# Layer-norm sums in float32r, gMLP weights converted ahead of time, and ten score units on half rows in an attention, feed-forward and gMLP kernel

## The chip, the core and the metric

The kernel runs on one core of a Trainium2 chip. Its time is the device time of one execution in microseconds, and a version is judged by the median of several runs. The profile is one execution of its own, recorded instruction by instruction.

## What is computed

Four batches of 448 tokens pass through soft-capped attention (12 heads of 64), a layer norm with a feed-forward part that is added to its input, and a gMLP block. All inputs and outputs are float32.

```python
scores = cap * tanh(scale * q @ k.T / cap)
x = (softmax(scores) @ v).transpose(0, 2, 1, 3).reshape(B, S, 768)
xn = (x - mean(x)) / sqrt(var(x) + 1e-06) * g_ln
x = x + relu(xn @ w_ch1) @ w_ch2                      # 768 -> 3072 -> 768
u, v = split(relu(x @ w_in))                          # 768 -> 512 + 512
v_n = (v - mean(v)) / sqrt(var(v) + 1e-06)
v_s = einsum('ts,bsd->btd', w_spatial, v_n) + b_spatial
out = (u * v_s) @ w_out                               # 512 -> 768
```

## The kernel before

**Precision.** A float32 matmul takes several passes of TensorE. For nearly all products the kernel instead splits both operands into a high and a low part in float32r and sums three matmuls (high by high, high by low, low by high; `mm3`, L547). The weights arrive as 64-bit numbers. `weight` (L566) loads one into a `w6` buffer, makes a float32 of it in a `wr` buffer (one step on ScalarE, three on VectorE), stores that in DRAM (`kept`) for the second use, and splits it into a `wh` buffer. There are two `w6`, two `wr` and three `wh` buffers. The second time the weight is used, the stored float32 is loaded and only split.

**Stages.** Work goes by pairs of batches. The lead computes attention of batches 0 and 1 with nothing else to do. Then come the feed-forward units of this pair, 24 hidden blocks in six groups: `h_units` (L977) make four hidden blocks per batch of 18 matmuls each, `y_units` (L989) add them to six output blocks, 12 matmuls each. Attention of batches 2 and 3 is spread between these units by `drive` (L1004) and `attend` (L1016). Then `gmlp` (L945) runs for the pair: products with `w_v` (`v_mm`, L846) and `w_u`, the spatial product (`sp_units`, L898) and the output product (`o_units`, L931). Feed-forward and gMLP of the second pair follow, with no attention beside them.

**Attention.** A unit is two heads, whose q and k (transposed) lie on partitions 0 to 63 and 64 to 127. `emit_s` (L643) makes the transposed scores of 128 keys at a time, in float32, one head on each half of the array's rows at the same time: chunks 0 and 1 together, chunk 2 later, each into a `two` tile (two banks of PSUM). The last 64 keys of two units are done together by `emit_st` (L656). ScalarE takes tanh and exp. `emit_v` (L705) multiplies with v and sums the exponentials, and `invert` (L676) passes these sums through DRAM to get reciprocals on all partitions. `emit_n` (L750) scales the result and adds it up in `acc`, from which the norm's mean is taken.

**Layer norm.** `ln_mean` (L769) sums `acc` over the partitions with a float32 matmul against ones, subtracts the mean, splits the centered values into `xn`, and adds up squares. `ln_scale` (L792) sums the squares by four small float32 matmuls (two instructions each) that write two columns, takes the root on GpSimd, and spreads the standard deviation over all partitions by DMA. x is multiplied by it before the products of `y_units` are added.

**Order.** All operations are first recorded, and `order` and `plan` (L251, L287) write out the order of every engine by simulating costs that are given in `Recorder`. An operation's due time is the amount of TensorE's work recorded before it, or, for others, that of its earliest user less a share of the way to it. A ready operation with the lowest due time goes first if the buffers it needs are free; none is started more than 28 us (`AHEAD`) before its due time. On the chip every engine then runs its own list in that order and waits where the plan was too optimistic. There are four `bank` and two `two` tiles for results of TensorE, 16 `rs`, 8 `rb`, 10 `hs` and 7 `es` buffers. All DMAs are issued on SP's queue.

Of the kernel before, what the change touches and what calls it, by code (L numbers as in the profile page):

```python
# [10 lines left out]
F32 = mybir.dt.float32  # L11
# [37 lines left out]

REBASE = 2.0 ** -112  # L50

EARLY = 2
# [410 lines left out]
def attn_ffn_gmlp_kernel(  # L463
# [49 lines left out]
    ones32 = const.tile([128, 2], F32, name="ones32")  # L513
    capt = const.tile([128, 1], F32, name="capt")
# [46 lines left out]
    def make(kind, j):  # L561

        with prog.early():
            made[kind, j] = weight(kind, j, [rs.get().rearrange("p a n -> p (a n)") for _ in range(2)])

    def weight(kind, j, home=None):  # L566
        if (kind, j) in made:
            return made.pop((kind, j))
# [7 lines left out]
        else:  # L576
# [5 lines left out]
            A.activation(out=t, in_=hi.bitcast(F32), func=ACTF.Copy, scale=REBASE)  # L582
# [7 lines left out]
            SP.dma_start(out=d, in_=t)  # L590
        if home:
            hi, lo = (x[:, 0:n] for x in home)
        else:
            o = (rb if j == 4 else rs).get()[:, :, 0:n] if kind == "ws" else wh.get()[:, :, 0:n]
            hi, lo = o[:, 0], o[:, 1]
        cp(hi, t, (A, V))
# [46 lines left out]
    def emit_s(i, cs):  # L643

        t = raws[i]
        scs = [twos.get()[:, :, 0:S] for _ in cs]
# [6 lines left out]
        for sc in scs:  # L653
            st.setdefault(i, []).append(expo(sc, es.get()))

# [112 lines left out]

    def ln_mean(b):  # L769

        ps = banks.get()[:, 0:S]
        T.matmul(out=ps, lhsT=ones32[:, 0:1].broadcast_to([128, 128]), rhs=accs[b % 2], start=True, stop=True)
        mean, sq = hs.get(), hs.get()
        A.activation(out=mean, in_=ps, func=ACTF.Copy, scale=1.0 / DM)
# [15 lines left out]
    def ln_scale(b):  # L792
        sq = ln.pop(b).rearrange("p (n c) -> p c n", c=NCT)
        ps = banks.get()
        with prog.group():
            for c in range(NCT):
                T.matmul(out=ps[0:CT, 2 * c:2 * c + 2], lhsT=sq[:, c], rhs=ones32, start=True, stop=True)
        var, rstd = (t[0:CT] for t in tok_t[b % 2])
        V.tensor_scalar(out=var, in0=ps[0:CT, 0:2 * NCT].rearrange("p (c t) -> p c t", t=2)[:, :, 0],
                        scalar1=1.0 / DM, scalar2=1e-6, op0=ALU.mult, op1=ALU.add)  # L800
# [45 lines left out]
    def v_mm(cs):  # L846

        two = [twos.get(), twos.get()]
        os = [banks.get() for _ in range(4)] + [t[:, j] for t in two for j in range(2)]
        os = os[:len(cs)]  # L850
        for k in range(KD):
            hi, lo = weight("wv", k)
            yh, yl = (t.rearrange("p a n -> p (a n)") for t in ysp[k])
            with prog.group():
                for c, o in zip(cs, os):
                    d = slice(c * 128, (c + 1) * 128)
                    for m, (l, r) in enumerate(((yh[:, d], hi), (yh[:, d], lo), (yl[:, d], hi))):
                        T.matmul(out=o, lhsT=l, rhs=r, start=(k == 0 and m == 0), stop=(k == KD - 1 and m == 2))
# [72 lines left out]
    def o_units(b, dt, ws):  # L931

        pss = [banks.get()[:, 0:S] for _ in ws]
        n = len(gs[b])
        with prog.group():
            for k, g in enumerate(gs[b]):
# [8 lines left out]
    def gmlp(bs, nxt):  # L945
# [16 lines left out]
        if nxt:  # L962
            ln_mean(first)
        vn.clear()
        for dts in ([0, 1, 2], *([dt] for dt in range(3, KD))):
            w = [weight("wo", dt) for dt in dts]
            for b in bs:
# [3 lines left out]
                else:  # L971
                    o_units(b, dts[0], w)
        gs.clear()
        if second:
            ln_mean(second)

    def h_units(bs, g, n):  # L977
# [3 lines left out]
        for m in steps:  # L981
            w = [weight("w1", j0 + j) for j in range(m)]
            j0 += m
            for b in bs:
                for j in range(m):
                    h_unit(b, w[j])
                    yield 3 * KD

    def y_units(bs, g, last):  # L989
# [3 lines left out]
        for b in bs:  # L993
            if b in ln:
                ln_scale(b)
# [20 lines left out]
    def attend(first, n, per):  # L1016
        todo = []
        for j in range(0, n, 2):
# [3 lines left out]
            stages = [(0.0, emit_s, i, (0, 1)), (0.1, emit_s, i, (2,)), (LOAD_QK, emit_load, i + 4),  # L1022
# [15 lines left out]
    def main():  # L1038
# [6 lines left out]
        P.memset(ones32, 1.0)  # L1045
        P.memset(mhalf, -0.5)
# [3 lines left out]
        lead = attend(0, 2 * H, 1.0) + [(H + 2.25, ln_mean, (0,)), (2 * H + 2.25, ln_mean, (1,))]  # L1050
# [73 lines left out]
```

## Time and profile before

| | |
|---|---|
| median of 3 runs | 1110.94 us (1109.65 to 1113.84) |
| the profiled execution | 1113.14 us, span of its instructions 1111.4 us |
| TensorE matmul, busy | 1094.4 us (98%), 5380 instructions |
| VectorE, busy | 704.7 us (63%) |
| ScalarE, busy | 415.6 us (37%) |
| mean granted clock of TensorE | 0.995 of full speed |

Engines are named PE (matmuls), PEld (weight loads, beside PE), DVE (VectorE), ACT (ScalarE), POOL (GpSimd) and SPq (the queue from which DMAs are issued). A row such as `bank<-rs,wh 128*128 128x448 f32` names the output tile, the operands' tiles, rows by columns of the array, and the moving operand; float32r operands are shown as f32 there. A float32 matmul stands as two instructions. All lines of the helper that records the operations are L455. Busy time counts an instruction from start to end; matmuls overlap, so the step from one start to the next is what one costs in a row.

### The profile page before, as it was taken

What the parts mean: (1) busy time and instruction counts of PE and PEld (TensorE: products, weight loads), DVE (VectorE), ACT (ScalarE), POOL (GpSimd) and SP (SyncE); (2) the same over time, 40 slices, a digit from 0 to 9 for tenths busy, and PEclk for the clock granted to TensorE, in tenths of its full rate; (3) what the DMA queues carried; (4) which work ended last, traced back from release to release, by engine and by line L of the source; (5) the groups of instructions that cost most, each with busy time, mean ns of one, the idle gap of its engine ahead of it and who ended that gap; (6) DMA issues with size and microseconds to landing.
All of it is one profiled execution on the core that took longest, in us unless ns stands there. A gap on an engine that the chain in (4) does not pass through costs nothing.

```text
span 1111.4 us, 14151 instructions
## 1 busy us (share of the span) xinstructions
PE 1094.4 (98%) x5380; PEld 899.6 (81%) x5380; DVE 704.7 (63%) x1183; ACT 415.6 (37%) x615; POOL 11.1 (1%) x17
## 2 busy tenths in 40 slices
PE   8989899999999999999999999999999999999998
PEld 2323597987888878978788899999999999998988
DVE  4768789676595776958989964533343433383861
ACT  7978743545334443354444440111111111120412
POOL 0000000000000000000001000000000000000100
PEclk9989999999999999999999999999999999999999
DMA  6545354555654564554475442212121212122303
GB/s 177 126 103 147 121 154 164 173 163 171 171 174 136 158 210 139 165 162 135 152 233 189 157 142 65 67 39 76 38 76 39 67 38 76 45 62 85 102 10 109
DMA packets 80128, 133.88 MB, mean 120 GB/s; under 512 B 35598, under 2 KB 47804, under 8 KB 80060
## 3 DMA queue, kind: packets, MB, share of 16 engines
q1 hardware_dynamic: 80060, 132.98, 40.0%
q8 instruction: 42, 0.69, 0.3%
q14 instruction: 26, 0.21, 0.1%
HBM read 100.91 MB, written 32.03 MB: 120 GB/s over the span
## 4 chain that ended last, share of the span: by engine, by line
PE 92%; DMA 4%; ACT 1%; SPq 1%; DVE 1%; issue 0%; DVEq 0%
PE bank L455 86%; PE two L455 6%; DMA inv<-rc 1%; DMA rc<-sum 1%; DMA hs<-inv 1%; SPq L455 1%; ACT es L455 1%; DMA qk<-in_qk_dram 1%; DMA w<-in_w_dram 1%; ACT hs L455 1%; DMA vt<-in_v_dram 0%; DVE acc L455 0%; DVE x L455 0%; DVE es L455 0%; ACT wr L455 0%
## 5 line engine op out<-in xcount | busy, mean ns | idle before, releaser
L455 PE MATMUL bank<-rs,wh 128*128 128x448 f32 x2232 | 451.5, 362 | 0.0
L455 PEld LDWEIGHTS bank<-rs,wh 128*128 128x128 f32 x2232 | 417.8, 187 | 33.6 <-ACT wr L455 2.8
L455 PE MATMUL bank<-rb,wh 128*128 128x448 f32 x1728 | 350.7, 363 | 0.0
L455 PEld LDWEIGHTS bank<-rb,wh 128*128 128x128 f32 x1728 | 324.8, 188 | 25.1 <-DVE hs L455 3.3
L455 DVE TENSOR_TENSOR x<-bank,x 128x448 f32<-128x448 f32 x144 | 89.5, 623 | 97.5 <-PE bank L455 96.5
L455 ACT ACTIVATE wh<-wr 128x512 fp32r<-128x512 f32 (+1 forms) x89 | 63.2, 710 | 207.4 <-PE bank L455 170.9
L455 ACT ACTIVATE rb<-bank 128x448 fp32r<-128x448 f32 x96 | 52.2, 544 | 222.4 <-PE bank L455 222.3
L455 DVE SCALAR_TENSOR_TENSOR rb<-bank,rb 128x448 fp32r<-128x448 f32 x96 | 59.8, 624 | 112.3 <-ACT rb L455 111.9
L455 DVE TENSOR_TENSOR wh<-wr,wh 128x512 fp32r<-128x512 f32 (+1 forms) x150 | 117.4, 782 | 10.7 <-ACT wh L455 6.0
L455 DVE SCALAR_TENSOR_TENSOR wr<-w,wr 128x512 int32<-128x512 int32 (+1 forms) x152 | 119.2, 785 | 2.2
L455 ACT ACTIVATE wr<-w 128x512 f32<-128x512 f32 (+1 forms) x76 | 57.6, 758 | 84.1 <-DVE wh L455 35.6
L455 ACT ACTIVATE es<-two,qsc 128x896 f32<-128x896 f32 x72 | 70.9, 1009 | 24.7 <-PE two L455 24.4
L455 PE MATMUL two<-qk 64*128 64x448 f32 x288 | 69.6, 584 | 4.2 <-DMA qk<-in_qk_dram 4.2
L455 ACT ACTIVATE es<-es,capt 128x896 f32<-128x896 f32 x72 | 72.2, 1043 | 0.0
L455 DVE CAST wh<-wr 128x512 fp32r<-128x512 f32 (+1 forms) x61 | 28.8, 472 | 66.0 <-PE bank L455 48.6
L455 PE MATMUL bank<-es,vt 128*64 128x448 f32 x288 | 63.8, 557 | 0.5 <-DMA vt<-in_v_dram 0.5
L455 PEld LDWEIGHTS two<-qk 64*128 64x128 f32 x288 | 25.0, 191 | 42.6 <-issue 22.3
L455 DVE TENSOR_TENSOR es<-es,es 128x896 f32<-128x896 f32 x48 | 52.0, 1083 | 3.5 <-ACT es L455 3.2
L455 PEld LDWEIGHTS bank<-es,vt 128*64 128x64 f32 x288 | 18.1, 137 | 41.1 <-issue 30.0
L455 ACT ACTIVATE hs<-bank 128x448 f32<-128x448 f32 x49 | 26.5, 541 | 64.2 <-PE bank L455 63.6
L455 DVE TENSOR_SCALAR wr<-wr 128x512 int32<-128x512 int32 (+1 forms) x76 | 35.8, 471 | 22.8 <-ACT wr L455 22.6
L455 PE MATMUL bank<-wh,rs 128*128 128x512 f32 x144 | 35.6, 395 | 0.0
(79 smaller groups left out, 620.0 us busy)
## 6 DMA issues: line engine op xcount, KB each, us to landing
w<-in_w_dram SPq DMA_DIRECT2D x24, 768.0 KB, 5.3
w<-in_w_dram SPq DMA_DIRECT2D x36, 512.0 KB, 4.1
qk<-in_qk_dram SPq DMA_DIRECT2D x48, 224.0 KB, 3.4
kept_w<-wr SPq DMA_DIRECT2D x24, 384.0 KB, 4.9
kept_w<-wr SPq DMA_DIRECT2D x36, 256.0 KB, 4.2
wr<-kept_w SPq DMA_DIRECT2D x24, 384.0 KB, 3.9
wr<-kept_w SPq DMA_DIRECT2D x36, 256.0 KB, 2.7
out_dram<-hs SPq DMA_DIRECT2D x24, 224.0 KB, 2.1
```

Of the source, the lines that this page charges most:

```text
L455: fn(*(put(a) for a in args), **{k: put(a) for k, a in kw.items()})
```

## The change

- Scores: from head 28 of 48 on (the last ten units of two heads), q and k are split into two float32r parts in `rs` buffers, and each chunk's scores are three float32r matmuls per head on half rows. Chunks 0, 1 and 2 are recorded directly behind one another, after the earlier unit's products with v; chunk 2 goes to two `bank` tiles.
- Layer norms: both sums over partitions are taken by `feature_sum`, which splits its input and does two float32r matmuls against a matrix of ones. The variance, now one row, passes through DRAM to the layout of the root. `ln_mean` is cut into the sum and `ln_center`; in the gMLP the first batch's follow the output product's first three columns, the second's sum the fifth. In the lead, batch 0's is recorded at 15.2 instead of 14.25 steps. `ln_scale` is recorded after a batch's second hidden block rather than before the y products.
- Weights: four instead of two weights of `w1` are made in the lead. The sixteen weights of the gMLP are turned into float32 and stored during 30 to 75% of the first pair's feed-forward units, so that its gMLP loads and splits them only.
- `v_mm` and `o_units`: other banks, and smaller groups for the planner. The first pair's first step has four hidden blocks a batch instead of three and one.

```diff
@@ -47,9 +47,16 @@
+AFTER = 0.3, 0.75, 0
+SPLIT = 14
+S_AT = 0.13, 0.14
 REBASE = 2.0 ** -112
-EARLY = 2
+EARLY = 4
@@ -511,6 +518,7 @@
+    onesr = const.tile([128, 128], F32R, name="onesr")
@@ -561,11 +569,17 @@
     def make(kind, j):
...
-            made[kind, j] = weight(kind, j, [rs.get().rearrange("p a n -> p (a n)") for _ in range(2)])
-    def weight(kind, j, home=None):
-        if (kind, j) in made:
-            return made.pop((kind, j))
+            made[kind, j] = weight(kind, j, [rs.get().rearrange("p a n -> p (a n)") for _ in range(2)]
+                                   if j < 2 else [t[:, i] for t in (wh.get(),) for i in range(2)])
+    def ahead(kind, j):
+        with prog.early():
+            value(kind, j)
+    def value(kind, j, home=None):
@@ -579,7 +593,12 @@
-            A.activation(out=t, in_=hi.bitcast(F32), func=ACTF.Copy, scale=REBASE)
+            with prog.either():
+                for e in (A, V) if home is None else (V, A):
+                    if e is A:
+                        A.activation(out=t, in_=hi.bitcast(F32), func=ACTF.Copy, scale=REBASE)
+                    else:
+                        V.tensor_scalar(out=t, in0=hi.bitcast(F32), scalar1=REBASE, scalar2=None, op0=ALU.mult)
@@ -588,12 +607,19 @@
+        return t
+    def weight(kind, j, home=None):
+        if (kind, j) in made:
+            return made.pop((kind, j))
+        n = width[kind]
+        t = value(kind, j, home)
...
-        cp(hi, t, (A, V))
+        cp(hi, t, (A, V) if home is None else (V, A))
@@ -643,6 +669,9 @@
     def emit_s(i, cs):
...
+        if i >= SPLIT * 2:
+            split_s(i, t, cs)
+            return
@@ -652,6 +681,37 @@
+    def split_s(i, t, cs):
+        if cs[0] == 0:
+            parts = [rs.get().rearrange("p a n -> p (a n)") for _ in range(2)]
+            raws["s", i] = parts
+            cp(parts[0], t, (A, V))
+            sub(parts[1], t, f(parts[0]))
+        hi, lo = raws["s", i]
+        for c in cs:
+            if c < 2:
+                two = twos.get()[:, :, 0:S]
+                sc = [two[:, half] for half in range(2)]
+            else:
+                sc = [banks.get()[:, 0:S] for _ in range(2)]
+            k = slice(S + 128 * c, S + 128 * c + 128)
+            with prog.group(0.1 if c == 1 else 0.2):
+                for m, (x, y) in enumerate(((hi, hi), (hi, lo), (lo, hi))):
+                    for half in range(2):
+                        r = slice(64 * half, 64 * half + 64)
+                        T.matmul(out=sc[half], lhsT=x[r, k], rhs=y[r, 0:S], start=m == 0, stop=m == 2)
+            e = es.get()
+            if c < 2:
+                st.setdefault(i, []).append(expo(two, e))
+            else:
+                for half in range(2):
+                    A.activation(out=e[:, half], in_=sc[half], func=ACTF.Tanh, scale=qsc)
+                A.activation(out=e, in_=e, func=ACTF.Exp, scale=capt)
+                st[i].append(e)
+        if 2 in cs:
+            del raws["s", i]
     def emit_st(i):
@@ -766,14 +826,28 @@
+    def feature_sum(ps, x):
+        t = rb.get()[:, :, 0:S]
+        cp(t[:, 0], x)
+        sub(t[:, 1], x, f(t[:, 0]))
+        with prog.group():
+            for j in range(2):
+                T.matmul(out=ps, lhsT=onesr, rhs=t[:, j], start=(j == 0), stop=(j == 1))
+    means = {}
     def ln_mean(b):
...
-        T.matmul(out=ps, lhsT=ones32[:, 0:1].broadcast_to([128, 128]), rhs=accs[b % 2], start=True, stop=True)
-        mean, sq = hs.get(), hs.get()
-        A.activation(out=mean, in_=ps, func=ACTF.Copy, scale=1.0 / DM)
+        feature_sum(ps, accs[b % 2])
+        means[b] = hs.get()
+        A.activation(out=means[b], in_=ps, func=ACTF.Copy, scale=1.0 / DM)
+    def ln_center(b):
+        mean, sq = means.pop(b), hs.get()
@@ -790,14 +864,14 @@
     def ln_scale(b):
-        sq = ln.pop(b).rearrange("p (n c) -> p c n", c=NCT)
-        ps = banks.get()
-        with prog.group():
-            for c in range(NCT):
-                T.matmul(out=ps[0:CT, 2 * c:2 * c + 2], lhsT=sq[:, c], rhs=ones32, start=True, stop=True)
+        ps = banks.get()[:, 0:S]
+        feature_sum(ps, ln.pop(b))
+        row = hs.get()[0:1]
+        V.tensor_scalar(out=row, in0=ps[0:1], scalar1=1.0 / DM, scalar2=1e-6, op0=ALU.mult, op1=ALU.add)
         var, rstd = (t[0:CT] for t in tok_t[b % 2])
-        V.tensor_scalar(out=var, in0=ps[0:CT, 0:2 * NCT].rearrange("p (c t) -> p c t", t=2)[:, :, 0],
-                        scalar1=1.0 / DM, scalar2=1e-6, op0=ALU.mult, op1=ALU.add)
+        d = dram.tile([1, S], F32, name=f"var_{b}")
+        SP.dma_start(out=d, in_=row)
+        SP.dma_start(out=var, in_=d.rearrange("a (n c) -> (a n) c", c=NCT))
@@ -846,16 +920,20 @@
     def v_mm(cs):
...
-        os = [banks.get() for _ in range(4)] + [t[:, j] for t in two for j in range(2)]
-        os = os[:len(cs)]
+        os = [t[:, j] for t in two for j in range(2)] + [banks.get() for _ in range(len(cs) - 4)]
...
-            with prog.group():
-                for c, o in zip(cs, os):
-                    d = slice(c * 128, (c + 1) * 128)
-                    for m, (l, r) in enumerate(((yh[:, d], hi), (yh[:, d], lo), (yl[:, d], hi))):
-                        T.matmul(out=o, lhsT=l, rhs=r, start=(k == 0 and m == 0), stop=(k == KD - 1 and m == 2))
+            for c, o in zip(cs, os):
+                if k in (0, KD - 1) or c == 0:
+                    part = ExitStack()
+                    part.enter_context(prog.group())
+                d = slice(c * 128, (c + 1) * 128)
+                for m, (l, r) in enumerate(((yh[:, d], hi), (yh[:, d], lo), (yl[:, d], hi))):
+                    T.matmul(out=o, lhsT=l, rhs=r, start=(k == 0 and m == 0), stop=(k == KD - 1 and m == 2))
+                if k in (0, KD - 1) or c == cs[-1]:
+                    part.close()
@@ -930,10 +1008,13 @@
     def o_units(b, dt, ws):
-        pss = [banks.get()[:, 0:S] for _ in ws]
+        pss = [banks.get()[:, 0:S]]
+        if len(ws) == 3:
+            two = twos.get()
+            pss += [two[:, j, 0:S] for j in range(2)]
         n = len(gs[b])
-        with prog.group():
-            for k, g in enumerate(gs[b]):
+        for k, g in enumerate(gs[b]):
+            with prog.group():
@@ -959,8 +1040,6 @@
-        if nxt:
-            ln_mean(first)
@@ -970,9 +1049,14 @@
+            if nxt and len(dts) > 1:
+                ln_mean(first)
+                ln_center(first)
+            elif second and dts[0] == KD - 2:
+                ln_mean(second)
...
-            ln_mean(second)
+            ln_center(second)
     def h_units(bs, g, n):
@@ -984,15 +1068,14 @@
+                    if b in ln and j == 1:
+                        ln_scale(b)
...
     def y_units(bs, g, last):
...
-        for b in bs:
-            if b in ln:
-                ln_scale(b)
@@ -1019,7 +1102,8 @@
-            stages = [(0.0, emit_s, i, (0, 1)), (0.1, emit_s, i, (2,)), (LOAD_QK, emit_load, i + 4),
+            stages = [(S_AT[0] if i >= 2 * SPLIT else 0.0, emit_s, i, (0, 1)),
+                      (S_AT[1] if i >= 2 * SPLIT else 0.1, emit_s, i, (2,)), (LOAD_QK, emit_load, i + 4),
@@ -1043,20 +1127,28 @@
+        V.tensor_copy(onesr, ones32[:, 0:1].broadcast_to([128, 128]))
...
-        lead = attend(0, 2 * H, 1.0) + [(H + 2.25, ln_mean, (0,)), (2 * H + 2.25, ln_mean, (1,))]
+        lead = attend(0, 2 * H, 1.0) + [(x, fn, (b,)) for x, b in ((H + 3.2, 0), (2 * H + 2.25, 1)) for fn in (ln_mean, ln_center)]
...
-                h_units(bs, g, 3 if g == 0 else 2), y_units(bs, g, g == NG - 1))))
+                h_units(bs, g, FG if g == 0 and p == 0 else 3 if g == 0 else 2), y_units(bs, g, g == NG - 1))))
             n = 2 * H if p + 1 < NP else 0
-            drive(units, attend(2 * H * (p + 1), n, 2 * NG * (FG * 3 * KD + KD * 3 * FG) / max(n, 1)))
+            total = NG * 2 * (FG * 3 * KD + KD * 3 * FG)
+            todo = []
+            if p == 0:
+                later = [("wv", k) for k in range(KD)] + [("wu", i) for i in range(KH)] + [("wo", k) for k in range(KD)]
+                later = later[AFTER[2]:]
+                for j, x in enumerate(later):
+                    todo.append((total * (AFTER[0] + (AFTER[1] - AFTER[0]) * j / len(later)), ahead, x))
+            drive(units, todo + attend(2 * H * (p + 1), n, 2 * NG * (FG * 3 * KD + KD * 3 * FG) / max(n, 1)))
```

## Rows read from the trace of the kernel before

**Rows 1.** Busy time by stretch of the span; the view's header names its columns.

```profile
core 0: us, PE busy (x) PEld busy (x) DVE busy (x) ACT busy (x) POOL busy (x), PEclk, DMA share, GB/s
...
14.60:70.00 55.40, 55.25 (x262) 17.99 (x266) 39.98 (x62) 52.23 (x66) 0.00 (x0) 1.00 0.53 126
...
70.00:129.00 59.00, 50.34 (x236) 23.46 (x228) 44.27 (x73) 41.70 (x58) 0.00 (x0) 0.94 0.43 116
...
243.00:434.00 191.00, 191.00 (x967) 156.69 (x966) 134.09 (x211) 78.91 (x111) 0.00 (x0) 1.00 0.55 165
...
533.00:653.00 120.00, 120.00 (x582) 102.53 (x581) 102.11 (x192) 53.46 (x92) 3.01 (x2) 1.00 0.58 192
...
653.00:667.00 14.00, 14.00 (x72) 13.12 (x71) 11.97 (x22) 8.43 (x16) 0.00 (x0) 1.00 0.12 36
...
684.45:687.86 3.41, 3.41 (x11) 3.03 (x10) 0.89 (x4) 0.00 (x0) 0.70 (x1) 0.50 0.31 78
```

**Rows 2.** TensorE's timeline, 74 to 131 us: start, length, instructions, [idle before <-releaser].

```profile
74.68 1.83 PE L455 MATMUL bank<-acc,ones 128*128 128x448 f32 x2 [4.12 <-DVE acc L455]
...
100.99 3.90 PE L455 MATMUL bank<-rs,rs 128*128 128x448 f32 x18 [1.57 <-ACT hs L455]
...
116.75 3.98 PE L455 MATMUL bank<-rs,rs 128*128 128x448 f32 x18 [0.87 <-ACT x L455]
...
129.04 1.02 PE L455 MATMUL bank<-acc,ones 128*128 128x448 f32 x2 [1.26 <-DVE acc L455]
```

**Rows 3.** TensorE's timeline, scores of one unit of two heads, 186 to 194 us.

```profile
186.57 1.77 PE L455 MATMUL two<-qk 64*128 64x448 f32 x8
...
188.27 2.48 PE L455 MATMUL bank<-es,vt 128*64 128x448 f32 x12
...
192.32 1.02 PE L455 MATMUL two<-qk 64*128 64x448 f32 x4
...
193.27 0.98 PE L455 MATMUL bank<-qk 64*64 64x448 f32 x8
```

**Rows 4.** TensorE's timeline, half rows of the spatial product, in three short windows.

```profile
605.47 0.68 PE L455 MATMUL bank<-rs,rb 64*128 64x448 f32 x4
...
605.47 0.88 PE L455 MATMUL bank<-rs,rb 64*128 64x448 f32 x6
...
606.28 0.47 PE L455 MATMUL bank<-rb,rb 128*128 128x448 f32 x1
```

**Rows 5.** VectorE's groups of instructions, shapes apart: count | busy us, mean ns.

```profile
L455 DVE SCALAR_TENSOR_TENSOR wr<-w,wr 128x512 int32<-128x512 int32 x96 | 65.9, 688 | 1.5
...
L455 DVE TENSOR_TENSOR es<-es,es 128x896 f32<-128x896 f32 x48 | 52.0, 1083 | 3.5 <-ACT es L455 3.2
...
L455 DVE SCALAR_TENSOR_TENSOR wr<-w,wr 128x768 int32<-128x768 int32 x56 | 53.3, 951 | 0.7
...
L455 DVE TENSOR_SCALAR wr<-wr 128x512 int32<-128x512 int32 x48 | 20.3, 422 | 13.1 <-ACT wr L455 13.1
```

**Rows 6.** TensorE's timeline, sums of the layer norms of batches 2 and 3.

```profile
602.80 0.91 PE L455 MATMUL bank<-acc,ones 128*128 128x448 f32 x2
...
603.21 3.15 PE L455 MATMUL bank<-rs,rb 128*128 128x448 f32 x15
...
680.54 3.26 PE L455 MATMUL bank<-ones,hs 128*112 128x2 f32 x16
```

**Rows 7.** TensorE's largest group of matmuls: count | busy us, mean ns.

```profile
L455 PE MATMUL bank<-rs,wh 128*128 128x448 f32 x2232 | 451.5, 362 | 0.0
```

**Rows 8.** ScalarE's first step of each conversion, by line, 243 to 434 us.

```profile
L455 ACT ACTIVATE wr<-w 128x512 f32<-128x512 f32 (+1 forms) x27 | 20.7, 765 | 25.8 <-DVE wh L455 13.9 <-DMA kept_w<-wr 10.7 <-DMA w<-in_w_dram 1.2
```

**Rows 9.** DMA issues on SP's queue, raw loads of `w_v` and `w_u`.

```profile
533.03 0.35 SPq L455 DMA_DIRECT2D w<-in_w_v_dram  x1
...
541.23 0.33 SPq L455 DMA_DIRECT2D w<-in_w_v_dram  x1
...
546.09 0.38 SPq L455 DMA_DIRECT2D w<-in_w_v_dram  x1
...
550.30 0.38 SPq L455 DMA_DIRECT2D w<-in_w_u_dram  x1
```

## Prediction

> **What bounds the kernel now.** I first read the stretches [rows 1]. From 243 us on TensorE is busy in all of the time in every stretch shown (191.00 of 191.00, 120.00 of 120.00, 14.00 of 14.00), while VectorE stands at 70% and 85%. So past the attention of batches 0 and 1 (the lead, up to about 129 us) a microsecond taken from TensorE's work is a microsecond of the span, and relief for any other engine is worth nothing there. The lead is another matter: from 70 to 129 us TensorE was busy 50.34 of 59.00 us, and its mean clock was 0.94. Its timeline [rows 2] says where the 8.66 us went: 4.12 us before the sum of batch 0's layer norm (it waited for `acc`), 1.57 and 0.87 us before units of the feed-forward part, 1.26 us before the second norm's sum, again for `acc`. The attention units in the feed-forward part and the few matmuls of the norms I read next, instruction by instruction.
>
> **Scores of the last ten pairs.** A unit of two heads spent 1.70 us on two chunks (186.57 to 188.27) and 0.95 on the third (192.32 to 193.27), 2.65 together, in float32 [rows 3]. The new form is nine pairs of half-row matmuls in float32r. The trace has that shape once: the spatial product's half rows, three pairs [rows 4]. From 605.47 to the next full-row matmul at 606.28 they take 0.81 us; the second pair's end lies 0.20 before the third's (0.68 and 0.88 from the common start). Nine pairs are then 0.81 + 6 x 0.20 = 2.01 us, entry and exit included. Saved: 0.64 us a unit, 6.4 us for ten. Bounds: if other work comes between the chunks, two more changes of row mode are paid, about 0.2 each (0.81 against three pairs at 0.20), leaving 0.24 x 10 = 2.4 us; the upper end is 7.
>
> A rule speaks against this. The Trainium skill, "TensorE: Matmul & The Clock Gate" (Part 3, The mechanism), has weight loads overlap matmuls in flight only where the row group differs. By it every next pair, on the same two row groups, would wait for its weights. The third pair of [rows 4] at 0.20 us speaks against that; what it would cost is a rival below.
>
> The price of it elsewhere: each unit gets a copy of 128x896 (ScalarE first) and a subtraction on VectorE; the nearest row is the 128x896 addition, 1.083 us [rows 5]. Tanh of the third chunk goes in two halves. These lie beside TensorE's work. The third chunk takes two of four `bank` tiles instead of one `two`: if ScalarE empties them late, the next unit waits. I put this into the term for stalls below.
>
> **Layer norms.** Each matmul against `ones32` that writes two columns costs 3.26 / 16 = 0.20 us [rows 6], as much as one with 448 columns (451.5 / 2232 = 0.202, [rows 7]), and there are 32 (eight a norm): 6.5 us. Eight of 0.20 take their place: 1.6. Saved 4.9. The sum for the mean is two float32 instructions; it lies between 0.40 us (to the next start, 602.80 to 603.21) and 0.91 (its record) [rows 6]; I take 0.75, as the instruction behind it started late as well. Two float32r matmuls are 0.40, so four norms save 1.4. Third, after the 16 two-column matmuls of the second pair the granted clock was 0.50 for 3.41 us (684.45 to 687.86, [rows 1]), that is 1.2 GHz, with nothing else unusual before it: half of that, 1.7 us, was lost. With four full-width matmuls in the place of the sixteen I expect no fall. Together 8.0 us; bounds 5 (the fall comes all the same, part of the work hid in the lead's idle time) and 8.5.
>
> What this adds: per sum a copy and a subtraction, hidden beside TensorE; for the variance a row on one partition and two more transfers on SP's queue, behind which later loads stand. It is started after the second unit of a batch, and at least two further units of 18 x 0.202 = 3.6 us lie before the products that need it, with four banks of 12 x 0.202 = 2.4 us behind; no stall expected. The first batch's centering comes later, after three of six output columns: 3 x 2 x 12 x 0.202 = 14.5 us of TensorE's work remain as its cover. The second batch's centering ran in 653 to 667 us beside 14.00 us of busy TensorE, with VectorE 11.97 busy [rows 1], so 14.5 hold one. I allow 0.5 us; without cover it would be up to 8.
>
> **The lead.** `acc` is waited for as before, but now a copy and a subtraction lie between it and the matmul, so the plan places the sum behind the next attention products, which TensorE can do meanwhile. And four weights of the first feed-forward units instead of two are ready early, so that up to two more units a batch (3.6 us each) can fill holes which now end on weights or `xn`. To be had: the 8.66 us of idle time and what the clock lost around the first stall (0.06 x 59 = 3.5 us, part of it while nothing ran; I count 2.8), 11.5 in all. I take 5.5 from the first stall and 1 from the rest: 6.5. Bounds: 11.5, and -4, as the two more weights put about 8 us on VectorE (2 x (0.56 + 3 x 0.95 + 0.56), a conversion and its split [rows 5]), which from 14.6 to 70 us is busy 39.98 of 55.40 beside a ScalarE at 94% [rows 1].
>
> **Weights of the gMLP converted early.** Sixteen conversions move from the gMLP into 30 to 75% of the first pair's feed-forward units, some 243 to 434 us by counting its matmuls. In the gMLP nothing is gained: TensorE was busy 120.00 of 120.00 there. On VectorE they cost 12 x (0.42 + 2 x 0.69) + 4 x (0.56, an estimate by width, + 2 x 0.95) = 31 us [rows 5], the subtractions of nine units 10: 134 + 41 = 175 of 191 us, 92%. That still fits (85% in the gMLP stopped nothing). The tighter resource are the raw buffers `w6` and `wr`, two each: 27 conversions were there [rows 8], now 43, one per 191 / 43 = 4.4 us. The pace of a buffer: loaded at 541.23, loaded again at 550.30, 9.07 us, or 4.5 a conversion with two buffers; the other, 533.03 to 546.09, 13.06 or 6.5, but then it waited for space [rows 9]. At 4.5 it is late by 43 x 4.5 - 191 = 3 us, and three `wh` buffers hold two weights ahead (one lasts 24 to 36 matmuls, 4.8 to 7.3 us, so 12 together). I take 3 us of small stalls, banks included; bounds 0 and 14. Each wait for a free buffer on SP's queue also holds the q, k and v loads behind it.
>
> The rest (groups by chunk in `v_mm` and `o_units`, other banks, four units in the first step) changes only order where TensorE is full: nothing, and a microsecond either way.
>
> **The sum.** -6.4 - 8.0 - 6.5 + 3 + 0.5 = -17.4. The profiled execution took 1113.14 us (span 1111.4, so 1.7 around it), giving 1095.7; it lies 2.2 above the median 1110.94, from which it would be 1093.5. I say 1095.
>
> **Rivals.**
> (a) The lead gives nothing: the plan again puts the sum where `acc` is late by the real transfers. For: the plan misjudged that once. Time 1095 + 6.5 = 1101.5; with more stalls 1104. Chance 0.16.
> (b) Slower: conversions outrun the buffers. The last buffers' rows allow 6.5 us a conversion; at 5.4 the 43 need 232 us, 41 more than there are, less 12 in stock: 29 us of waiting TensorE, 1095 - 3 + 29 = 1121. It is slower than before from (191 + 12 + 19) / 43 = 5.2 us a conversion. Against: pace 4.5, and VectorE has 8% left. Chance 0.06.
> (c) The half rows don't overlap their weight loads: each pair at about 0.31 instead of 0.20 (0.81 less 0.20 for the third pair leaves 0.61 for the first and the exit [rows 4]), so 2.01 + 8 x 0.11 = 2.9 a unit, 0.25 more than now: 1095 + 6.4 + 2.5 = 1104. By the rule of the Trainium skill named above it would go this way. Chance 0.04.
> (d) The chunks don't stay in a row: 1095 + 4 = 1099. Chance 0.08.
> (e) Everything in the lead is had and no stall comes: 1087 or below. Chance 0.06.
>
> **How the numbers follow.** The forecast, 1089 to 1100, has 0.60. Cases (a), (c), (d) and (e) lie within 1086 to 1106, which leaves out (b) and the far ends. A measurement of this kernel can tell about 0.5%, 5.6 us, from no change: faster is below 1105.4. That is all but (b), half of (c) and of the far end of (a): faster 0.87, same 0.07, slower 0.06.
>
> **What would show it.** Right: the scores' nine pairs take about 2.0 us in each of ten units, next to one another; no two-column matmuls and no clock of 0.50 near the second pair's first products; less idle TensorE than 8.66 us between 70 us and the end of the lead; TensorE full from there, VectorE above 90% in the 243 to 434 stretch. Wrong: pairs 0.3 apart; waits of TensorE for `wh` or for banks in that stretch, or for `rs` at the second pair's start; a new fall of the clock behind a stall. The forecast fails above all if such stalls reach 10 us.

## The result and the profile after

The changed kernel takes 1101.06 us, median of 4 runs (1099.58 to 1104.36), the kernel before 1112.39 (1109.65 to 1114.38) beside it. The ratio is 0.9906, with a 95% interval from 0.9877 to 0.9935: between 7 and 14 us less. The profiled execution took 1101.24 us, its span 1099.3. So it is faster, as forecast, by 11.3 us rather than 17.4. 1101.06 lies a microsecond above the 1089 to 1100 to which the forecast gave 0.60, and within the wider 1086 to 1106. It is also close to the 1101.5 of rival (a), in which the lead gives nothing; the rows below say that this is a coincidence, as the lead did give something.

Stretches of the changed kernel's trace, to set beside [rows 1] (the later ones begin 8 or 9 us earlier, as the work before them takes less time):

```profile
core 0: us, PE busy (x) PEld busy (x) DVE busy (x) ACT busy (x) POOL busy (x), PEclk, DMA share, GB/s
...
14.60:70.00 55.40, 54.97 (x258) 18.01 (x254) 46.08 (x72) 51.91 (x66) 0.00 (x0) 1.00 0.60 165
70.00:129.00 59.00, 54.44 (x261) 28.04 (x260) 49.82 (x86) 43.42 (x63) 1.94 (x1) 0.97 0.40 107
234.00:427.00 193.00, 190.53 (x996) 160.66 (x996) 164.32 (x262) 89.33 (x129) 0.00 (x0) 0.99 0.70 228
525.00:645.00 120.00, 119.46 (x582) 102.57 (x581) 80.55 (x157) 39.55 (x71) 3.02 (x2) 1.00 0.39 119
```

Two things differ from before. Between 70 and 129 us TensorE idles 4.56 us instead of 8.66. And in the stretch of the early conversions, which was full, it now idles 2.47 us. There the clock fell too. TensorE's timeline around the longest of these waits, and ScalarE's beside it:

```profile
404.65 4.57 PE L462 MATMUL bank<-rs,wh 128*128 128x448 f32 x22
410.75 0.68 PE L462 MATMUL bank<-rs,wh 128*128 128x448 f32 x2 [1.53 <-ACT wh L462]
411.95 6.36 PE L462 MATMUL bank<-rs,wh 128*128 128x448 f32 x23 [0.52 <-DVE wh L462]
```

```profile
404.44 0.90 ACT L462 ACTIVATE wr<-w 128x768 f32<-128x768 f32 x1 [2.35 <-DMA w<-in_w_dram]
...
408.64 0.89 ACT L462 ACTIVATE wr<-w 128x768 f32<-128x768 f32 x1 [1.01 <-DMA w<-in_w_dram]
409.44 0.52 ACT L462 ACTIVATE rb<-bank 128x448 fp32r<-128x448 f32 x1
409.87 0.83 ACT L462 ACTIVATE wh<-wr 128x768 fp32r<-128x768 f32 x1
```

```profile
411.75:415.16 3.41, 3.21 (x9) 2.89 (x10) 3.38 (x7) 2.02 (x4) 0.00 (x0) 0.50 0.10 37
```

TensorE waits for the high part of a weight (`wh`), which ScalarE makes at 409.87. ScalarE runs its list in order, and ahead of that step stands the first step of the next weight's conversion (`wr<-w`, 408.64), which itself had waited 1.01 us for a raw load. The split's own input was ready before that, when VectorE ended the conversion at 408.32:

```profile
406.38 1.94 DVE L462 SCALAR_TENSOR_TENSOR wr<-w,wr 128x768 int32<-128x768 int32 x2
```

Started then, the high part would have been done at 409.15 (0.83 us later), before TensorE's work ran out at 409.22. (This takes it that a `wh` buffer was free by then, which the trace does not tell.) Behind the two waits the granted clock is 0.50 (1.2 GHz) for 3.41 us, and half of that, 1.7 us, is lost as well.

The scores of one unit, to set beside [rows 3], from TensorE's timeline:

```profile
217.29 0.47 PE L462 MATMUL two<-rs 64*128 64x448 f32 x2
217.60 0.56 PE L462 MATMUL two<-rs,rs 64*128 64x448 f32 x4
218.00 0.37 PE L462 MATMUL two<-rs 64*128 64x448 f32 x2
218.21 0.57 PE L462 MATMUL two<-rs,rs 64*128 64x448 f32 x4
218.61 0.36 PE L462 MATMUL bank<-rs 64*128 64x448 f32 x2
218.81 0.57 PE L462 MATMUL bank<-rs,rs 64*128 64x448 f32 x4
219.31 1.88 PE L462 MATMUL bank<-rb,wh 128*128 128x448 f32 x8
```

Nine pairs from 217.29 to 219.31: 2.02 us, all three chunks in a row. Eight of the ten units take this; the others take 2.24 and 2.37.

### The profile page after: what moved, and what is told of

It is laid out like the page before. It is cut to its first block, busy times and chain, and to the rows that moved or that the text cites. A ratio compares the mean times of both kernels' runs of the same rounds, so it can differ in the third digit from the quotient of the medians.

```text
span 1099.3 us, 14352 instructions
## 1 busy us (share of the span) xinstructions
PE 1082.9 (99%) x5416; PEld 901.0 (82%) x5416; DVE 730.1 (66%) x1234; ACT 406.9 (37%) x611; POOL 11.7 (1%) x17
## 4 chain that ended last, share of the span: by engine, by line
PE 81%; DMA 9%; DVE 5%; ACT 2%; issue 1%; SPq 1%; ACTq 0%; DVEq 0%
PE bank L462 75%; PE two L462 6%; DMA w<-in_w_dram 4%; DVE wr L462 2%; DMA hs<-inv 2%; SPq L462 1%; DVE es L462 1%; DMA w<-in_w_out_dram 1%; DMA inv<-rc 1%; ACT es L462 1%; DMA wr<-kept_w 1%; DMA w<-in_w_u_dram 1%; ACT wr L462 1%; DVE x L462 0%; DMA rc<-sum 0%
## 5 line engine op out<-in xcount | busy, mean ns | idle before, releaser
L462 PE MATMUL bank<-rs,wh 128*128 128x448 f32 x2184 | 445.9, 363 | 3.0 <-ACT wh L462 1.5
L462 PEld LDWEIGHTS bank<-rs,wh 128*128 128x128 f32 x2184 | 410.0, 188 | 34.6 <-issue 1.9
L462 ACT ACTIVATE wr<-w 128x512 f32<-128x512 f32 (+1 forms) x54 | 40.9, 758 | 86.1 <-DMA w<-in_w_dram 49.3
L462 ACT ACTIVATE es<-two,qsc 128x896 f32<-128x896 f32 x62 | 61.6, 1016 | 13.8 <-PE two L462 13.6
L462 PE MATMUL two<-qk 64*128 64x448 f32 x168 | 41.9, 597 | 4.4 <-DMA qk<-in_qk_dram 4.3
L462 PEld LDWEIGHTS two<-qk 64*128 64x128 f32 x168 | 15.0, 195 | 29.6 <-ACT es L462 11.5
L462 DVE TENSOR_TENSOR x<-x,hs 128x448 f32<-128x448 f32 x36 | 21.6, 618 | 25.2 <-DMA hs<-inv 15.6
```

The lines of the kernel that those rows point to most:

```text
L462: fn(*(put(a) for a in args), **{k: put(a) for k, a in kw.items()})
```

## Experiments

All times are medians beside the kernel before, which had medians from 1110.99 to 1111.65 in these comparisons; ratios are to it, with their 95% intervals.

### Which part makes TensorE wait: early conversion and scores, each on its own

Three kernels form a square with the changed kernel: early conversion of the gMLP's weights on or off, scores in float32r or float32.

**Without early conversion.**

```diff
-                later = later[AFTER[2]:]
+                later = []
```

> The changed kernel without the early conversion of the sixteen gMLP weights; they are converted in the first gMLP, as before the change. Theory (early conversion crowds the raw buffers and causes the waits of TensorE for wh in the 234 to 427 us stretch and the clock fall behind them, 4.5 us): those go, the gMLP stays full, about 1096.5 us where the changed kernel has 1101. Rival (the early conversion pays, as the gMLP and the later centering need VectorE): waits of 5 us or more appear between 525 and 660 us, 1101 to 1106. Second rival (the stalls come from the score parts' extra work): the stalls at 340 and 409 us stay, 1101.

Measured: 1096.85 us (1094.19 to 1099.38), ratio 0.9879 (0.986 to 0.9898). Its stretches:

```profile
234.00:427.00 193.00, 193.00 (x1023) 163.36 (x1023) 145.54 (x229) 79.63 (x115) 0.00 (x0) 1.00 0.53 165
525.00:645.00 120.00, 120.00 (x586) 103.40 (x585) 107.43 (x203) 52.93 (x94) 2.64 (x2) 1.00 0.57 193
645.00:659.00 14.00, 14.00 (x72) 13.11 (x71) 12.05 (x23) 6.84 (x13) 1.01 (x1) 1.00 0.07 21
```

TensorE is full in all three. The conversions back in the first gMLP put VectorE at 107.43 of 120 us and stop nothing, and the later centering of the norms doesn't need the relief either. The forecast of 1096.5 holds: the early conversion buys nothing, and here it costs 4.2 us by the medians and 3.0 by the ratios, whose intervals overlap.

**Scores in float32, early conversion kept.**

```diff
-SPLIT = 14
+SPLIT = 99
```

> The changed kernel with all scores in float32 at the old places; everything else as changed. Theory (the score parts save TensorE's work, 20.8 us for ten units where they were 26.6): 1101 + 6 = 1107 us, stalls in 234 to 427 us stay. Rival (the parts' copies, subtractions and banks cause the stalls of 4.5 us): stalls go, 1102 to 1103.

Measured: 1101.35 us (1098.79 to 1104.14), ratio 0.9922 (0.9904 to 0.9939). Nearest to the rival's 1102 to 1103, not the theory's 1107: the waits are gone.

```profile
234.00:427.00 193.00, 193.00 (x977) 158.59 (x976) 164.93 (x271) 79.22 (x112) 0.00 (x0) 1.00 0.70 234
```

VectorE and the DMA engines are as busy as in the changed kernel (164.93 and 164.32 us, 0.70 both), and yet TensorE is full. So the load of these two does not decide. ScalarE's is not the same: 79.22 us in 112 instructions, against 89.33 in 129. In the changed kernel the first step of a conversion (`wr<-w`) may go to ScalarE or VectorE, and in this stretch the planned order gives ScalarE 34 of 41 with float32r scores and 27 of 43 with float32. So its load, its order and the scores' precision change together here.

**Neither.** Both edits at once.

> The changed kernel with neither the early conversion of the gMLP weights nor float32r scores (scores in float32 at the old places). With the three runs on hand (both 1101.1, early conversion alone 1101.35, scores alone 1096.85) this is the fourth corner. Theory (each is harmless alone and only both together make TensorE wait): early conversion alone neither costs nor gains, so this is 1101.3, and the scores in float32r are worth 4.5. Rival (the early conversion costs some 4 us in any case and the scores nothing): 1097.

Measured: 1101.30 us (1100.13 to 1101.75), ratio 0.99 (0.9882 to 0.9919). The square is closed:

| | scores float32 | scores float32r |
|---|---|---|
| no early conversion | 1101.30 | 1096.85 |
| early conversion | 1101.35 | 1101.06 |

By the medians early conversion alone costs nothing, float32r scores alone are worth some 4.5 us, and together the one takes back what the other gives. The ratios, each to the kernel before beside it, do not show this: 0.9900 and 0.9879 without early conversion, 0.9922 and 0.9906 with it, so that it costs 2.4 us in one column and 3.0 in the other, and the intervals overlap. That it takes both rests on the traces, one execution of each kernel. Of the four, only the kernel with both lets TensorE wait after the lead for more than 0.4 us. And the traces can be compared by stage: from the start to the last product of the first group of `y_units` (the 144th matmul `bank<-rb,wh`), from there to the gMLP's first product with `w_v`, and from there to the end, in us:

| traced execution | start to first group | to the gMLP | to the end | span |
|---|---|---|---|---|
| kernel before | 182.7 | 361.6 | 567.1 | 1111.4 |
| norms alone (below) | 178.8 | 361.6 | 564.0 | 1104.4 |
| neither | 175.9 | 361.6 | 562.5 | 1100.0 |
| early conversion alone | 174.4 | 361.6 | 562.8 | 1098.7 |
| float32r scores alone | 175.6 | 355.4 | 562.6 | 1093.6 |
| both: the changed kernel | 175.2 | 360.9 | 563.2 | 1099.3 |
| both, two-column sums (below) | 177.8 | 359.0 | 565.7 | 1102.5 |
| scores alone, old places (below) | 176.2 | 358.5 | 562.3 | 1097.0 |

The middle stage is 361.6 in all four kernels with float32 scores, to 0.02 us, so that it can be read closely. Early conversion alone changes nothing there, float32r scores alone take 6.2 us off, and both together 0.7. Of the 5.5 us between the last two, 2.47 are waits, 1.7 the clock and some 0.5 the two slower units of scores; 0.8 are not traced.

**Three `wr` buffers.** One `hs` buffer pays for it.

```diff
-COUNTS = 16, 8, 10, 3, 2, 2, 3, 7, 2, 1
+COUNTS = 16, 8, 9, 3, 2, 3, 3, 7, 2, 1
```

> The changed kernel with three wr buffers instead of two, paid for by nine hs buffers instead of ten. Theory (conversions wait for buffers): one more lets the raw weights run ahead, the waits for wh in 234 to 427 us go, 1097. Rival (the raw loads themselves take 7 us, beside the other transfers, and w6 or the DMA engines hold them up): waits stay, 1101.

Measured: 1102.96 us (1098.67 to 1107.14), ratio 0.9919 (0.9895 to 0.9943). TensorE still waits, once and for longer, now here (ScalarE's timeline, then TensorE's):

```profile
387.24 0.89 ACT L462 ACTIVATE wr<-w 128x768 f32<-128x768 f32 x1 [3.15 <-DMA w<-in_w_dram]
388.04 0.62 ACT L462 ACTIVATE wh<-wr 128x512 fp32r<-128x512 f32 x1
```

```profile
388.70 0.74 PE L462 MATMUL bank<-rb,wh 128*128 128x448 f32 x1 [2.66 <-ACT wh L462]
```

The same pattern, plainer: ScalarE stands 3.15 us at a step that waits for a raw load, and directly behind it in its list is the split for which TensorE waits 2.66. That split's input was ready at 386.41, when VectorE ended the conversion:

```profile
385.75 0.66 DVE L462 SCALAR_TENSOR_TENSOR wr<-w,wr 128x512 int32<-128x512 int32 x1
```

So the order alone delayed it by 1.63 us, to 388.04. A third buffer for converted weights doesn't remove the waits. With nine `hs` buffers the lead lost time as well (TensorE idles 5.25 us from 70 to 129 us, at a mean clock of 0.94), so the total says little.

**Early conversions spread out.**

```diff
-AFTER = 0.3, 0.75, 0
+AFTER = 0.05, 0.95, 0
```

> The changed kernel with the sixteen early conversions spread over 5 to 95% of the first pair's feed-forward units rather than 30 to 75%: one more conversion each 24 us instead of each 12. Theory (crowded buffers): at most one short wait for wh, no clock fall, about 1097 us. Rival (score parts cause the stalls): the stalls stay, 1101.

Measured: 1107.82 us (1104.41 to 1113.93), ratio 0.9978 (0.9963 to 0.9993). Worse by 7 us, where I expected better by 4. So fewer conversions at a time don't remove the waits. (The spread also begins earlier; which of its places hurts most isn't told apart.) The trace is of the slowest of the twelve executions, 1113.93 us, so a usual one probably waits less than the 6.4 us that it shows in the middle stage. One of these waits, on ScalarE and then on TensorE:

```profile
334.66 0.85 ACT L462 ACTIVATE wh<-wr 128x768 fp32r<-128x768 f32 x1 [4.91 <-DVE wr L462]
335.42 0.52 ACT L462 ACTIVATE hs<-bank 128x448 f32<-128x448 f32 x1
335.84 1.15 ACT L462 ACTIVATE hs<-bank,qsc 128x448 f32<-128x448 f32 x2
```

```profile
335.08 0.57 PE L462 MATMUL two<-rs,rs 64*128 64x448 f32 x4
335.99 0.46 PE L462 MATMUL bank<-rs 64*128 64x448 f32 x1 [0.34 <-ACT hs L462]
337.68 0.47 PE L462 MATMUL bank<-rs 64*128 64x448 f32 x1 [1.22 <-DVE hs L462]
```

ScalarE stands 4.91 us at a split whose conversion VectorE has not finished. Behind it queue the steps that empty `bank` tiles, and TensorE waits for these with the third chunk, which needs two of the four.

**Chunks at their old places**, with and without early conversion.

```diff
-S_AT = 0.13, 0.14
+S_AT = 0.0, 0.1
```

> The changed kernel without early conversion (1096.85), with the float32r scores recorded at the float32 form's old places: two chunks before, the third behind the products with v. Theory (by the steps of [rows 4], each change of row mode costs about 0.2 and there is one entry and exit more): +2 to +4 us, 1099 to 1101. Rival (places don't matter, the row change is hidden): 1097.

> The changed kernel with the float32r scores at the old places, the early conversion kept. Theory (three chunks in a row plus the last keys' scores ask for four banks and for ScalarE in one burst, and with early conversion this delays the splits of weights): the waits near 341 and 409 us go, but the row changes come: 1100 to 1102. Rival (the burst is not the cause, the raw loads are): waits stay, 1103 to 1105.

Measured without early conversion: 1099.78 us (1098.87 to 1100.95), ratio 0.9891 (0.9874 to 0.9907), by the medians 2.9 more than in a row (1.3 by the ratios, whose intervals overlap). With it: 1104.16 (1102.14 to 1107.4), ratio 0.9934 (0.9916 to 0.9952). The first from TensorE's timeline:

```profile
215.27 0.47 PE L462 MATMUL two<-rs 64*128 64x448 f32 x2
...
216.69 2.48 PE L462 MATMUL bank<-es,vt 128*64 128x448 f32 x12
...
219.85 0.47 PE L462 MATMUL bank<-rs 64*128 64x448 f32 x2
...
220.65 11.68 PE L462 MATMUL bank<-rb,wh 128*128 128x448 f32 x57
```

1.42 and 0.80 us make 2.22 a unit, 0.2 more than in a row: 2 us for ten units. Between the traces the middle stage is 3.1 us longer, with no wait, within the 2 to 4 expected. With early conversion the waits stay without the burst of three chunks (three for `wh`, 1.5 us together, and two for ScalarE's steps that empty banks, 1.9). So the burst is not what causes them, as the rival had it; that the raw loads are, this run does not show. The longest of these waits, 1.30 us, ends when ScalarE has emptied the two banks of a third chunk. ScalarE began that at 473.98, right behind the chunk's matmuls (473.96), so no late load stands in front there: it is the shortage of banks that the prediction named.

### The layer norms

**The norms alone, in the kernel before.**

```diff
-        T.matmul(out=ps, lhsT=ones32[:, 0:1].broadcast_to([128, 128]), rhs=accs[b % 2], start=True, stop=True)
+        feature_sum(ps, accs[b % 2])
...
                     h_unit(b, w[j])
+                    if b in ln and j == 1:
+                        ln_scale(b)
```

> The kernel before with one change: the norms' sums in float32r, started after a batch's second hidden block. Theory: 4.9 of two-column matmuls, 1.4 of float32 sums and 1.7 of the clock, 8 us less, of which a part may hide in the lead: 1103 to 1105 where the kernel before takes 1111. Rival (the clock falls in another place, or the two transfers more delay the products): 1107 or more.

Measured: 1106.45 us (1105.28 to 1108.6), ratio 0.9964 (0.995 to 0.9978): 4.6 us less by the medians, 4.0 by the ratio, not 8. The mean granted clock is 1.000 in the traced execution, so the fall behind the second pair's sums is gone, and the one in the lead with it:

```profile
core 0: 1104.4 us, clock 1.000
```

Waits that remain, or are new, stand in the lead and at the second pair's first sum:

```profile
70.00:129.00 59.00, 52.48 (x257) 23.93 (x253) 50.50 (x85) 46.86 (x68) 1.75 (x1) 1.00 0.44 124
```

```profile
617.62 0.36 PE L455 MATMUL bank<-rb,onesr 128*128 128x448 f32 x1
619.22 0.47 PE L455 MATMUL bank<-rb,onesr 128*128 128x448 f32 x1 [1.24 <-DVE rb L455]
```

TensorE still idles 6.52 us in the lead, and the second matmul of a sum waits 1.24 us for the low part that VectorE makes, a step I had costed at nothing. In the changed kernel the same sum has its two matmuls without a wait:

```profile
627.42 0.57 PE L462 MATMUL bank<-rb,onesr 128*128 128x448 f32 x2
```

The table by stage puts 3.9 us of this kernel's gain before the first group of `y_units` and 3.1 behind the gMLP's start, 7.0 together; the traced execution of the kernel before was 2.2 us slower than its median, which makes this total too large.

**Two-column sums in the changed kernel, at the new place.** The variance is summed by `ones32` as before the change, and its two transfers through DRAM go.

```diff
-        feature_sum(ps, ln.pop(b))
...
+        sq = ln.pop(b).rearrange("p (n c) -> p c n", c=NCT)
...
+            for c in range(NCT):
+                T.matmul(out=ps[0:CT, 2 * c:2 * c + 2], lhsT=sq[:, c], rhs=ones32, start=True, stop=True)
...
```

> The changed kernel with the variance's sum again by eight float32 matmuls of two columns a norm, at the new place after the second hidden block. Theory: 32 of them at 0.20 instead of 8 at 0.20, +4.8 us, and if the clock falls behind them as before another 1.7: 1106 to 1107.5. Here they stand in two groups of eight with hidden units between for the second pair, so no fall is as possible as one. Rival (they hid in idle time and only the fall counted): 1101 to 1103.

Measured: 1104.96 us (1103.3 to 1106.72), ratio 0.9953 (0.9938 to 0.9967), 3.9 more than the changed kernel by the medians and 5.2 by the ratios: between the theory's range and the rival's, and near the theory's 4.8 without a fall. The second pair's two groups and the stretch around them:

```profile
651.49 1.61 PE L462 MATMUL bank<-ones,hs 128*112 128x2 f32 x8
...
663.85 1.61 PE L462 MATMUL bank<-ones,hs 128*112 128x2 f32 x8
```

```profile
640.00:700.00 60.00, 60.00 (x300) 56.46 (x301) 40.93 (x74) 17.80 (x33) 2.65 (x2) 1.00 0.27 81
```

1.61 us for eight is the old price, and with hidden units between the groups the clock stays at 1.00 in this execution. So the 1.7 us that the clock gave back may be owed to the new place as well as to the new form. By stage this kernel is 2.6 us behind the changed one up to the first group of `y_units`, and 2.5 behind it from the gMLP on: as far as one trace of each can tell, every pair's sixteen matmuls cost their 0.20 us in full, in the lead too.

### The lead

All three on the kernel without early conversion (1096.85).

**The first sum later**, at 16.07 or 16.22 steps instead of 15.2 (the edit for the first; the second has `H + 4.22`).

```diff
-        lead = attend(0, 2 * H, 1.0) + [(x, fn, (b,)) for x, b in ((H + 3.2, 0), (2 * H + 2.25, 1)) for fn in (ln_mean, ln_center)]
+        lead = attend(0, 2 * H, 1.0) + [(x, fn, (b,)) for x, b in ((H + 4.07, 0), (2 * H + 2.25, 1)) for fn in (ln_mean, ln_center)]
```

> The changed kernel without early conversion of the gMLP weights (1097 us), and with the first layer norm's sum recorded at 16.07 instead of 15.2 steps of the lead, behind the next unit's first scores and its predecessor's first products with v. Theory (TensorE stands 2.8 us before this sum, and the clock falls behind that, 1.4 us, only because the sum is too early in its list): most of the 4.3 us go, 1093. Rival (the wait moves to the first feed-forward units, whose input comes later): holes between 95 and 130 us grow by as much, 1097.

> As the run before, with the sum at 16.22 steps, behind all products of that unit with v. Theory: no wait before the sum at all and no clock of 0.50 near it, 1092.5, or 1 us more if the first feed-forward units wait. Rival (the wait moves): 1097.

Measured: 1095.8 (1093.01 to 1098.13) and 1096.18 (1094.02 to 1096.88), ratios 0.9863 (0.9843 to 0.9883) and 0.9864 (0.9848 to 0.988). Neither can be told from 0.9879. In the later one the waits before the first sum shrink and new ones stand before the second (TensorE's timeline):

```profile
77.65 0.47 PE L462 MATMUL bank<-rb,onesr 128*128 128x448 f32 x1 [1.15 <-ACT rb L462]
79.11 0.62 PE L462 MATMUL bank<-rb,onesr 128*128 128x448 f32 x1 [0.99 <-DVE rb L462]
...
121.10 0.47 PE L462 MATMUL bank<-rb,onesr 128*128 128x448 f32 x1 [1.27 <-ACT rb L462]
```

The wait moves: the rival holds.

**Two weights ready instead of four.**

```diff
-EARLY = 4
+EARLY = 2
```

> The changed kernel without early conversion of the gMLP weights (1097 us), with two instead of four weights of the feed-forward part ready in the lead, as before the change. Theory (four ready weights fill the holes at the lead's end): the holes of 3.4 us between 100 and 150 us come back in place of 0.7, 1099.5. Rival (they are filled anyway, or the weights' work on VectorE slows the lead): 1096 to 1097.

Measured: 1098.38 us (1097.9 to 1098.88), ratio 0.9886 (0.987 to 0.9901): 1.5 more by the medians, within the intervals. A hole before the first feed-forward unit is back, which is 0.40 in the changed kernel:

```profile
100.88 3.36 PE L462 MATMUL bank<-rs,rs 128*128 128x448 f32 x15 [1.38 <-DVE hs L462]
```

So the four weights probably bring a part of the lead's gain; the size is not settled.

## Why the prediction was right, and where its sizes were off

**What bounds the kernel.** Right: what came off TensorE's list past the lead came off the span, and relief for VectorE in the gMLP was worth nothing (the run without early conversion).

**By stage.** The terms of the sum can be set beside the table of traces. Up to the first group of `y_units`, where the lead (6.5) and half of the norms' matmuls (3.15) fall, 9.65 us were forecast and 7.5 measured. In the middle stage, scores less stalls, it was 3.4 and 0.7. From the gMLP on (the other half of the norms, the clock, less 0.5 for centering) it was 4.35 and 3.9. These sum to 12.1 between the two traced executions, where the medians give 11.3.

**Scores.** The step from three pairs to nine was right to a hundredth: 2.01 expected, 2.02 measured in eight units, and the ten take 20.8 us where they took 26.6. The half rows do overlap their weight loads, over nine pairs and not only three, and rival (c) is refuted: the steps within the nine are 0.20 us. The rule of the Trainium skill, "TensorE: Matmul & The Clock Gate" (Part 3, The mechanism), that weight loads overlap matmuls in flight only where the row group differs, does not hold for these pairs at 0.20 us. The same section also has a load run ahead into the background weight buffer, and the prediction left that out. In the kernel without early conversion the ten units take 20.3 us, 6.3 less than before. But the term was booked apart from the stalls, and in the changed kernel the two belong together: 6.2 us alone in the middle stage, 0.7 beside the early conversions.

**Layer norms.** 8.0 expected; alone they gave 4.6 by the medians. The clock's fall behind the second pair's sums went as forecast. What the prediction had wrong for the norms alone is that the copy and subtraction cost nothing: they are the last thing the second pair's first sum waits for (1.24 us). How much of the first pair's part hid in the lead, where TensorE still idles 6.52 us, stays open. In the changed kernel that wait is not there, and the run with two-column sums shows their price in full at both places (2.6 and 2.5 us, forecast 2.45 each).

**The lead.** 6.5 expected. From 70 to 129 us idle time fell by 4.1 us. The clock stood at 0.50 for 6.82 us before (73.47 to 80.29), in 1.21 of which TensorE was idle, and for 3.41 after (77.25 to 80.66), so that it gave back 2.8 less 1.7, or 1.1: together 5.2. The first stage's 7.5 us, less the 3.15 forecast for the norms, leave 4.4. So the lead gave some 4 to 5. The split was wrong. The first stall, from which I expected 5.5, went only from 4.12 to 3.01 us:

```profile
75.97 0.47 PE L462 MATMUL bank<-rb,onesr 128*128 128x448 f32 x1 [2.82 <-DVE rb L462]
76.63 0.47 PE L462 MATMUL bank<-rb,onesr 128*128 128x448 f32 x1 [0.19 <-DVE rb L462]
...
98.70 3.98 PE L462 MATMUL bank<-rs,rs 128*128 128x448 f32 x18 [0.40 <-DVE hs L462]
...
113.61 3.92 PE L462 MATMUL bank<-rs,rs 128*128 128x448 f32 x18 [1.04 <-DVE x L462]
```

The holes behind it gave more than the 1 us I took: of 1.57, 0.87 and 1.26 [rows 2], 0.40 and 1.04 are left. That the two errors partly cancel is luck.

**Early conversion.** This is the term that was mis-sized most. The stalls were put at 3 us; between the traces with and without early conversion the middle stage differs by 5.5, of which 2.47 are waits and 1.7 the clock. Another 0.54 us stand near the end of the first gMLP, where the prediction allowed 0.5 for centering. The place and the event (waits for `wh` and a new fall of the clock) were named, but the mechanism was only half right. I reckoned with buffers by their number and rate; VectorE stood at 85%, not 92%, a third buffer didn't remove the waits, and fewer conversions at a time made it worse. In the waits shown above (three kernels), the last thing TensorE waits for is a step of ScalarE, or one of VectorE after it, and ScalarE has stood at a step that waits for a late raw load or a late conversion. That is read from the traces; no run changes ScalarE's order alone, and one wait above (1.30 us, for banks) is of another kind. Why the float32 form, with the same load on VectorE and the DMA engines, escapes it is not settled: ScalarE has 10 us less to do there and takes fewer of the first steps, order and stock differ by a microsecond or two, and no run here isolates any of these.

**The sum.** 17.4 forecast, 11.3 measured by the medians. Of what is missing, the traces put about half in the middle stage (the stalls above all, and 0.6 of the scores), most of the rest in the lead, and 0.5 behind. All three errors have the same sign. The kernel without early conversion, at 1096.85 us, is better than both, a gain of 14.1 by the medians.

## What to carry to other kernels

When one engine is full, a change that takes work off it pays by its start-to-start price (here 6.2 us for the scores where 6.4 were forecast, as long as nothing else stalled), and a row of the same shape elsewhere in the trace gives that price well. Work moved ahead of time must be needed at its old place: check there first whether the full engine ever waits, and leave it if not. And don't cost background work by busy shares alone: an engine that runs its list in order passes one late load on to everything behind it, so look for what stands behind each step that can wait.

## What the runs showed of the hardware that I had not expected

Spreading the same sixteen conversions thinner made the kernel 7 us slower, though it lowers the DMA load where they were dense (207 GB/s against 228 in 234 to 427 us; ahead of that, from 150 to 240 us, it is 191 against 174). A fall of the clock to 0.50 for 3.41 us followed two waits of 1.53 and 0.52 us close together in the changed kernel, but the kernel with two-column sums has waits as long at the same place and keeps 1.00:

```profile
400.00:415.00 15.00, 12.89 (x64) 11.15 (x61) 10.57 (x16) 11.27 (x17) 0.00 (x0) 1.00 0.75 242
```

So the same event brings the fall in one execution and not in another, and a microsecond or two of the difference between two single traces can be that alone.
